# Another order list for all engines and the DMA queue, and one sigmoid ahead of the branch, in an mLSTM + feed-forward kernel

## The chip, the cores and the metric

One core of one Trainium2 chip runs the kernel. The metric is device time in microseconds (us), as the median of runs; lower is better.

## The reference

Two stages follow each other. The first is a gated recurrence over 768 time steps for 4 batches x 8 heads with head size 40: at each step a running maximum `m`, a 40x40 state `C` and a vector `n` are updated and read out.

```
m_new = maximum(f[t] + m, i[t])
C = exp(f[t] + m - m_new) * C + exp(i[t] - m_new) * outer(v[t], k[t])
n = exp(f[t] + m - m_new) * n + exp(i[t] - m_new) * k[t]
y[t] = sigmoid(o[t]) * (C @ q[t]) / maximum(abs(n . q[t]), 1)
```

The second is a feed-forward layer on the 3072 x 320 result: `h = x @ w_in` (320 x 2048), a rational function of each element, `g = (a0 + a1 h + a2 h^2 + a3 h^3) / (1 + |b0||h| + |b1| h^2 + 1e-6)`, and `g @ w_out` (2048 x 320). The weights arrive as 64-bit floats; the kernel splits each of them into a high and a low part on the chip.

## The kernel before

**The work.** The recurrence is cut into 24 units (768 steps in 6 blocks of 128, for each of 4 batches). Two units make one pair, and each pair gives 256 rows of the feed-forward input, a block. There are 12 blocks (n = 0 to 11). The feed-forward work of a block is cut into 8 steps (i = 0 to 7), each with 256 of the 2048 hidden columns. Blocks 0 and 1 are done in two halves: steps 0 to 3 of both, then steps 4 to 7 of both, so that the weights of the second half may arrive later.

**The order.** Every piece of work is registered in a plan with a name, an engine, the names that it reads and writes, and a cost. A text constant, `ORDER`, names all 2723 pieces in one sequence. `plan.listed` turns it into indices and asserts that each piece comes after those it depends on and that no ring of buffers overflows; `plan.issue` then emits them. Within one engine the instructions keep the order of the list (`_Queue` ties each to the one before it), and all loads and nearly all stores go through one DMA queue (SP), in list order too. Across engines only the data dependencies and the reuse of buffers make one wait for another.

**The names.** For a weight chunk `i0..i7`, `o0..o7`, `j0`, `j1` (parts of w_in, w_out, and the last 64 rows of w_in): `raw` is the load; `s0`, `s2`, `o0` are ScalarE steps, `s1`, `s3` VectorE steps, `o2` GpSimd steps of the split; `oc` copies a part of `j` to other partitions through the DMA queue. For a unit u: `lk`, `lq`, `lv` load k, q, v, `lf`, `la` load decay factors that were stored before (units 4 on; units 0 to 3 get them from TensorE, `pf`, `pa`, `pc`); `ogl` loads the output gate and `og` is its sigmoid (ScalarE, three pairs in one go); `kp`, `ke`, `d0`, `d1` are GpSimd, `tk`, `tq`, `S`, `ow` TensorE, `ek`, `eq` ScalarE, `sc` (a scan), `qa`, `P`, `u0`, `u1` VectorE steps. For a pair: `it`, `i1`, `xt` TensorE, `ab`, `xh` ScalarE, `rc`, `x`, `xl` VectorE, `g` GpSimd. For a feed-forward step `n_i`: `f1`, `f2`, `f3` TensorE, `ha`, `u`, `p1`, `y`, `r0` ScalarE, `p3`, `gh`, `m`, `gl` VectorE, `w`, `rm` GpSimd; `ev` and `ed` write the block out. `early` and `gate` are the gate preprocessing (mostly VectorE), of the first 256 time steps and of the rest; `squares`, `lx` and `li` belong to it. `hot` is one of 90 matmuls of the identity by itself, whose results nobody reads. A suffix `.k` is the k-th piece of that name.

**The branch.** The program exists in two variants; a flag is computed from `moe_a` ahead of a branch (`_prologue`, `_decide`), and all of the list is inside the branch. The inputs here take the first variant.

The helper that ties the instructions of a queue has line 34, so nearly all rows of the profile have that line.

Of the kernel before, what the change touches and what calls it, by code (L numbers as in the profile page):

```python
# [147 lines left out]
early early.1 le early.2 early.3 hot hot.1 hot.2 hot.3 hot.4 hot.5 hot.6 hot.7 hot.8 hot.9 hot.10 hot.11 hot.12 hot.13  # L148
hot.14 hot.15 hot.16 hot.17 raw_o1 s2_o1 early.4 zero early.5 early.6 early.7 early.8 early.9 early.10 s0_o1.1
early.11 mc early.12 early.13 early.14 early.15 early.16 early.17 eye1 early.20 early.21 gate.2 gate.4 gate.5 li.2 eye  # L150
s0_o1 s1_o1 s3_o1 li.1 hot.18 s1_o1.1 s3_o1.1 lk_0 pf_0 early.18 raw_i6 gate.6 sc_0 hot.19 hot.20 hot.21 raw_o0 hot.22
pa_0 hot.23 s2_i6 hot.24 hot.25 hot.26 hot.27 s2_o0 s0_o0 o0_o1 s1_o0 hot.28 hot.29 zero.2 s3_o0 s0_o0.1 pa_1 s1_o0.1
s3_o0.1 li.3 lv_0 raw_j1 o2_o1 s0_i6 hot.30 hot.31 hot.32 early.19 ogl_4 gate.3 hot.33 hot.34 ogl_2 s1_i6 squares lx.2
raw_i4 o0_o0 hot.35 hot.36 s0_i4 s2_i4 pc_0 kp_0 tk_0 ke_0 pc_1 s0_j1 s1_i4 o2_o0 hot.37 hot.38 zero.3 s3_i4 o0_i4
ek_0 hot.39 hot.40 hot.41 hot.42 hot.43 zero.1 hot.44 hot.45 hot.46 hot.47 lq_0 hot.48 hot.49 hot.50 raw_o5 hot.51
hot.52 hot.53 hot.54 hot.55 hot.56 o2_i4 hot.57 hot.58 hot.59 hot.60 hot.61 s2_j1 s1_j1 s3_i6 raw_i2 lk_1 raw_j0 s0_o5
kp_1 li s3_j1 ogl_0 o0_i6 s0_o5.1 lq_1 s1_o5 lx.1 hot.62 tq_0 hot.63 s2_o5 eq_0 s1_o5.1 hot.64 o0_j1 hot.65 hot.66
pa_2 ogl_3 o2_i6 lx.3 s3_o5.1 s3_o5 o0_o5 S_0 tk_1 hot.67 qa_0 P_0 P_0.1 lx s0_j0 pc_2 ogl_5 raw_i0 ow_0 pf_1 gate.7
u0_0 ek_1 gate.21 lv_1 hot.68 tq_1 s1_j0 o2_j1 hot.69 hot.70 hot.71 d1_0 ogl_1 lk_2 o2_j1.1 sc_1 s2_j0 s3_j0 eq_1
s0_i2 hot.72 hot.73 hot.74 s2_i2 hot.75 S_1 ke_1 qa_1 o2_o5 o0_j0 o2_j0 raw_i3 u1_0 P_1 s1_i2 P_1.1 hot.76 pf_2 s0_i0  # L160
s1_i0 raw_i1 s2_i0 og_0 o2_j0.1 gate.1 ow_1 gate s3_i2 it_0 s3_i0 u0_1 d1_1 it_0.1 i1_0 hot.77 ab_0 ab_0.1 lq_2 hot.78
hot.79 hot.80 hot.81 sc_2 s0_i3 rc_0 kp_2 u1_1 s1_i3 tk_2 hot.82 g_0 x_0 o0_i0 o0_i2 g_0.1 ke_2 s2_i3 s3_i3 x_0.1
hot.83 hot.84 hot.85 hot.86 hot.87 hot.88 hot.89 ek_2 s2_i1 pf_3 s0_i1 s1_i1 s3_i1 xt_0 o2_i0 oc_j0 xh_0 xl_0 tq_2
eq_2 xh_0.1 o0_i1 o0_i3 S_2 lk_3 xl_0.1 raw_o3 lv_2 kp_3 tk_3 f1_0_0 f1_0_0.1 P_2 P_2.1 ek_3 s0_o3 s2_o3 o2_i1 lf_4
lq_3 ow_2 qa_2 sc_3 o2_i2 ha_0_0 s1_o3 s0_o3.1 pa_3 s3_o3 u0_2 d1_2 ke_3 u_0_0 s1_o3.1 s3_o3.1 p1_0_0 p3_0_0 u1_2
w_0_0 tq_3 eq_3 S_3 P_3 y_0_0 r0_0_0 P_3.1 lk_4 f1_0_1 sc_4 kp_4 tk_4 pc_3 raw_o2 gh_0_0 ek_4 m_0_0 oc_j1 f1_0_1.1
f1_0_2 qa_3 s0_o2 s0_o2.1 raw_i7 rm_0_0 s1_o2 s2_o2 ha_0_1 o2_i3 u_0_1 s1_o2.1 p1_0_1 s0_i7 s3_o2 s2_i7 w_0_1 gl_0_0
s3_o2.1 f2_0_0 f2_0_0.1 lv_3 ow_3 u0_3 p3_0_1 it_1 it_1.1 y_0_1 lq_4 s1_i7 s3_i7 i1_1 f1_0_2.1 d1_3 ke_4 raw_o7 ab_1
ab_1.1 rc_1 f3_0_0 tq_4 r0_0_1 gh_0_1 u1_3 o0_o3 ha_0_2 g_1 x_1 m_0_1 f3_0_0.1 f2_0_1 f1_0_3 gate.8 p1_0_2 g_1.1
p3_0_2 eq_4 x_1.1 rm_0_1 s2_o7 la_4 qa_4 u_0_2 w_0_2 gate.9 gl_0_1 f1_0_3.1 ha_0_3 p1_0_3 raw_i5 lk_5 lf_5 kp_5 d0_4  # L170
S_4 P_4 P_4.1 y_0_2 p3_0_3 f2_0_1.1 f3_0_1 f3_0_1.1 u_0_3 sc_5 r0_0_2 gh_0_2 w_0_3 gate.10 lq_5 tk_5 xt_1 xh_1 la_5
ek_5 m_0_2 xl_1 tq_5 xh_1.1 xl_1.1 rm_0_2 o0_o2 eq_5 qa_5 gl_0_2 ke_5 S_5 P_5 lv_4 ow_4 y_0_3 o0_i7 r0_0_3 u0_4 f1_1_0
P_5.1 gh_0_3 o2_i7 s0_o7 s1_o7 d1_4 u1_4 raw_o4 s0_o4 s2_o4 s3_o7 s1_o4 s0_o7.1 o2_o2 f1_1_0.1 f1_1_1 ha_1_0 o2_o3
f1_1_1.1 s1_o7.1 p1_1_0 s3_o4 s3_o7.1 d0_5 s2_i5 s0_o4.1 f2_0_2 f2_0_2.1 f3_0_2 f3_0_2.1 f2_0_3 m_0_3 rm_0_3 u_1_0
w_1_0 p3_1_0 s1_o4.1 ha_1_1 p1_1_1 u_1_1 s0_i5 gate.11 s3_o4.1 lv_5 lk_6 gate.12 lk_7 gl_0_3 gate.13 f1_1_2 kp_6 w_1_1
p3_1_1 s1_i5 f2_0_3.1 gate.18 s3_i5 f3_0_3 f3_0_3.1 o0_o4 y_1_0 o2_o4 r0_1_0 gh_1_0 pe_0_3 ow_5 pe_0_3.1 u0_5 f1_1_2.1
ha_1_2 m_1_0 tk_6 d1_5 ek_6 f2_1_0 f2_1_0.1 gate.14 gate.15 p1_1_2 u1_5 rm_1_0 gate.16 it_2 it_2.1 gate.19 o0_i5 lq_6
o2_i5 y_1_1 gl_1_0 gate.17 u_1_2 w_1_2 i1_2 p3_1_2 gate.20 ab_2 la_6 ab_2.1 rc_2 r0_1_1 gh_1_1 lf_6 y_1_2 f3_1_0 m_1_1
f1_1_3 f1_1_3.1 ha_1_3 tq_6 sc_6 f3_1_0.1 g_2 x_2 eq_6 r0_1_2 gh_1_2 qa_6 f2_1_1 rm_1_1 u_1_3 p1_1_3 gl_1_1 m_1_2
f2_1_1.1 f1_0_4 f1_0_4.1 f1_0_5 raw_o6 ogl_10 g_2.1 lf_7 ogl_8 o0_o7 s2_o6 ha_0_4 x_2.1 f3_1_1 p1_0_4 p3_1_3 p3_0_4  # L180
ke_6 S_6 P_6 lq_7 w_1_3 f1_0_5.1 f3_1_1.1 P_6.1 u_0_4 y_1_3 rm_1_2 gl_1_2 r0_1_3 s0_o6.1 gh_1_3 kp_7 s1_o6.1 w_0_4
ha_0_5 p1_0_5 m_1_3 gate.24 p3_0_5 s3_o6.1 rm_1_3 gl_1_3 f1_0_6 f2_1_2 f1_0_6.1 f2_1_2.1 u_0_5 w_0_5 y_0_4 ha_0_6
r0_0_4 u_0_6 y_0_5 f3_1_2 f3_1_2.1 f2_1_3 f2_1_3.1 gh_0_4 m_0_4 f3_1_3 f3_1_3.1 r0_0_5 pe_1_3 d0_6 pe_1_3.1 p1_0_6
gate.25 f1_0_7 f1_0_7.1 xt_2 rm_0_4 f2_0_4 gh_0_5 f2_0_4.1 gl_0_4 f3_0_4 ha_0_7 xh_2 xh_2.1 f3_0_4.1 f1_1_4 u_0_7
f2_0_5 f2_0_5.1 p3_0_6 xl_2 xl_2.1 m_0_5 o2_o7 w_0_6 s0_o6 s1_o6 tk_7 f1_1_4.1 s3_o6 y_0_6 p1_0_7 p3_0_7 w_0_7 f1_1_5
f1_1_5.1 rm_0_5 o0_o6 o2_o6 r0_0_6 gh_0_6 gl_0_5 m_0_6 y_0_7 ha_1_4 ek_7 p1_1_4 r0_0_7 p3_1_4 f3_0_5 u_1_4 gh_0_7
gate.22 gate.23 f3_0_5.1 tq_7 f2_0_6 f2_0_6.1 f1_1_6 rm_0_6 gl_0_6 f3_0_6 w_1_4 ha_1_5 p1_1_5 eq_7 y_1_4 m_0_7 rm_0_7
lk_8 lv_6 ogl_9 lq_8 la_7 ogl_6 gate.26 sc_7 qa_7 r0_1_4 gh_1_4 f3_0_6.1 f2_0_7 f2_0_7.1 f1_1_6.1 gl_0_7 u_1_5 ha_1_6
S_7 ke_7 P_7 P_7.1 ow_6 u_1_6 p1_1_6 w_1_5 f3_0_7 f3_0_7.1 m_1_4 p3_1_5 y_1_5 r0_1_5 rm_1_4 ev_0_7 w_1_6 f1_1_7
f1_1_7.1 f1_2_0 ha_1_7 u_1_7 p3_1_6 y_1_6 ev_0_7.1 r0_1_6 gl_1_4 u0_6 kp_8 d1_6 f2_1_4 f2_1_4.1 f3_1_4 f3_1_4.1  # L190
f1_2_0.1 d0_7 gh_1_5 u1_6 m_1_5 gh_1_6 m_1_6 lv_7 gate.27 rm_1_5 gl_1_5 f2_1_5 f2_1_5.1 tk_8 p1_1_7 ha_2_0 u_2_0 w_1_7
w_2_0 ek_8 p1_2_0 p3_1_7 ow_7 u0_7 it_3 d1_7 it_3.1 y_1_7 r0_1_7 p3_2_0 i1_3 y_2_0 f3_1_5 f3_1_5.1 lk_9 lf_8 ogl_11
u1_7 ed_0_7 ogl_7 ed_0_7.1 la_8 ab_3 ab_3.1 f1_2_1 gh_1_7 m_1_7 f1_2_1.1 rm_1_6 gl_1_6 rm_1_7 tq_8 rc_3 f2_1_6
f2_1_6.1 f3_1_6 f3_1_6.1 og_6 gl_1_7 g_3 sc_8 f2_1_7 ke_8 x_3 f2_1_7.1 g_3.1 ha_2_1 p1_2_1 f3_1_7 eq_8 qa_8 u_2_1
w_2_1 r0_2_0 p3_2_1 y_2_1 x_3.1 gh_2_0 S_8 P_8 f3_1_7.1 f1_2_2 f1_2_2.1 kp_9 m_2_0 ev_1_7 r0_2_1 ev_1_7.1 gh_2_1 tk_9
m_2_1 ek_9 ha_2_2 rm_2_0 gl_2_0 p1_2_2 p3_2_2 lq_9 lf_9 rm_2_1 gl_2_1 lv_8 la_9 f1_2_3 f1_2_3.1 ha_2_3 p1_2_3 p3_2_3
tq_9 f2_2_0 eq_9 u_2_2 u_2_3 w_2_2 y_2_2 r0_2_2 qa_9 P_8.1 f2_2_0.1 sc_9 w_2_3 gh_2_2 y_2_3 r0_2_3 m_2_2 f3_2_0 ke_9
lf_10 lk_10 d0_8 f1_2_4 f1_2_4.1 f1_2_5 ha_2_4 f3_2_0.1 rm_2_2 f2_2_1 f1_2_5.1 p1_2_4 ha_2_5 S_9 f2_2_1.1 P_9 P_9.1
f3_2_1 gh_2_3 lv_9 f3_2_1.1 xt_3 f2_2_2 gl_2_2 xh_3 kp_10 xh_3.1 f2_2_2.1 f3_2_2 tk_10 f3_2_2.1 f2_2_3 m_2_3 xl_3
xl_3.1 u_2_4 rm_2_3 ek_10 p1_2_5 w_2_4 gl_2_3 ow_8 ow_9 u0_8 d1_8 p3_2_4 u_2_5 y_2_4 it_4 it_4.1 d0_9 f2_2_3.1 u1_8  # L200
u0_9 p3_2_5 f3_2_3 i1_4 r0_2_4 w_2_5 ab_4 sc_10 gh_2_4 m_2_4 ab_4.1 f1_2_6 y_2_5 r0_2_5 f3_2_3.1 f1_2_6.1 rc_4 ha_2_6
gh_2_5 d1_9 u1_9 g_4 x_4 ed_1_7 ogl_16 rm_2_4 gl_2_4 u_2_6 f2_2_4 f2_2_4.1 p1_2_6 p3_2_6 m_2_5 lk_11 lk_12 f1_2_7
# [1271 lines left out]
```

## Time and profile before

| | us |
|---|---|
| median of 3 runs (501.81 to 502.59) | 501.81 |
| profiled execution | 500.23 |
| span from its first to its last instruction | 498.4 |

The profile is of one execution on the chip. The rows that the prediction rests on stand in a section of their own below.

### The profile page before, as it was taken

How to read it: one execution, taken by the hardware profiler on the slowest of the kernel's cores; microseconds unless marked ns; L12 is line 12 of the kernel's file. 1: busy time of each engine (PE TensorE's matmuls, PEld its weight loads, DVE VectorE, ACT ScalarE, POOL GpSimd, SP SyncE). 2: the span in 40 equal slices, each digit the busy share in tenths (PEclk: the TensorE clock that was granted, in tenths of full speed). 3: DMA queues.
4: the chain of work that ended last, by engine and by line, in shares of the span. 5: the costliest groups of instructions: out<-in, count | busy, mean ns of one | idle time of the engine just before them, and what ended most of it. 6: DMA issues, size and time to landing. Idle time of an engine off the chain costs nothing.

```text
span 498.4 us, 14219 instructions
## 1 busy us (share of the span) xinstructions
PE 478.1 (96%) x5631; PEld 462.1 (93%) x5631; DVE 421.9 (85%) x716; ACT 402.5 (81%) x698; POOL 385.8 (77%) x365
## 2 busy tenths in 40 slices
...
GB/s 181 221 178 238 229 208 177 103 9 71 113 106 77 59 83 101 99 75 83 44 83 87 131 70 57 60 77 15 29 115 62 2 75 3 11 19 1 27 1 35
DMA packets 120158, 42.54 MB, mean 85 GB/s; under 512 B 104338, under 2 KB 112594, under 8 KB 120082
## 3 DMA queue, kind: packets, MB, share of 16 engines
...
## 4 chain that ended last, share of the span: by engine, by line
PE 73%; DVE 7%; ACT 5%; DMA 4%; issue 3%; POOL 3%; SPq 3%; DVEq 0%; ACTq 0%; POOLq 0%
PE ph L34 30%; PE po L34 29%; PE y L34 4%; PE kq L34 3%; PE ow L34 3%; SPq L34 2%; PE ps L34 2%; DMA kr<-in_k_dram 2%; POOL p L34 2%; PE px L34 1%; DMA rawo<-in_moe_w_out_dram 1%; ACT ph L34 1%; DMA rawi<-in_moe_w_in_dram 1%; DVE w L34 1%; DVE gH L34 1%
## 5 line engine op out<-in xcount | busy, mean ns | idle before, releaser
L34 POOL TENSOR_TENSOR p<-p,w 128x512 f32<-128x512 f32 (+1 forms) x97 | 127.8, 1318 | 59.7 <-DVE w L34 55.8
L34 PE MATMUL ph<-xk,wi 128*128 128x256 f32 x1152 | 167.9, 282 | 0.6 <-DVE zo L34 0.5
L34 PEld LDWEIGHTS ph<-xk,wi 128*128 128x128 f32 x1152 | 150.0, 188 | 1.9 <-PE ph L34 0.7
L34 POOL TENSOR_TENSOR w<-w,ha 128x512 f32<-128x512 f32 (+1 forms) x97 | 127.3, 1318 | 9.9 <-ACT w L34 9.9
L34 PE MATMUL po<-wo,gH 128*128 128x320 f32 x768 | 134.6, 312 | 0.0
L34 PEld LDWEIGHTS po<-wo,gH 128*128 128x128 f32 x768 | 115.1, 188 | 0.8
L34 DVE SCALAR_TENSOR_TENSOR gL<-p,ps,ph 128x512 fp32r<-128x512 f32 (+1 forms) x97 | 71.3, 735 | 22.0 <-POOL p L34 19.9
L34 DVE SCALAR_TENSOR_TENSOR w<-w,gH 128x512 f32<-128x512 f32 (+1 forms) x97 | 81.7, 843 | 4.0
L34 ACT ACTIVATE ph<-w,cd 128x512 f32<-128x512 f32 (+1 forms) x97 | 66.6, 687 | 22.6 <-POOL w L34 12.2
L34 DVE SCALAR_TENSOR_TENSOR gH<-p,ps,ph 128x512 fp32r<-128x512 f32 (+1 forms) x97 | 71.3, 735 | 13.8 <-ACT ph L34 12.8
L34 ACT ACTIVATE w<-ha,ba 128x512 f32<-128x512 f32 (+1 forms) x97 | 78.6, 812 | 2.3
L34 ACT ACTIVATE ha<-ph 128x512 f32<-128x512 f32 (+1 forms) x97 | 57.5, 593 | 27.4 <-PE ph L34 26.6
L34 PE MATMUL po<-wo,gL 128*128 128x320 f32 x384 | 77.2, 314 | 0.8 <-DVE gL L34 0.8
L34 DVE SCALAR_TENSOR_TENSOR p<-p,ps,ph 128x512 f32<-128x512 f32 (+1 forms) x97 | 70.5, 734 | 7.2 <-ACT p L34 7.0
L34 ACT ACTIVATE p<-ph,ps 128x512 f32<-128x512 f32 (+1 forms) x97 | 65.3, 680 | 0.3
L34 PEld LDWEIGHTS po<-wo,gL 128*128 128x128 f32 x384 | 59.2, 188 | 2.4 <-DVE gL L34 1.8
L34 ACT ACTIVATE ph<-ph 128x512 f32<-128x512 f32 (+1 forms) x97 | 56.0, 578 | 2.2
L34 PE MATMUL ph<-xk,wY 128*128 128x256 f32 x192 | 53.6, 279 | 0.0
L34 PE MATMUL ph<-xk,wj 128*128 128x256 f32 x192 | 53.4, 278 | 0.0
L34 PEld LDWEIGHTS ph<-xk,wj 128*128 128x128 f32 x192 | 36.2, 188 | 0.0
L34 PEld LDWEIGHTS ph<-xk,wY 128*128 128x128 f32 x192 | 36.1, 188 | 0.0
L34 PE MATMUL hot<-ident 128*128 128x128 f32 x180 | 24.9, 296 | 4.0 <-DVE flag_out L370 4.0
...
## 6 DMA issues: line engine op xcount, KB each, us to landing
rawo<-in_moe_w_out_dram SPq DMA_DIRECT2D x8, 640.0 KB, 6.0
ab<-scrA SPq DMA_DIRECT2D x40, 128.0 KB, 3.6
rawi<-in_moe_w_in_dram SPq DMA_DIRECT2D x8, 512.0 KB, 5.5
...
vb<-in_v_dram SPq DMA_DIRECT2D x48, 80.0 KB, 3.5
og<-in_o_gate_dram SPq DMA_DIRECT2D x48, 80.0 KB, 3.4
...
out_dram<-ot SPq DMA_DIRECT2D x47, 80.0 KB, 2.2
```

The costliest lines, as they stand in the source:

```text
L34: made = fn(*args, **kwargs)
```

## The change

`ORDER` is replaced as a whole by another sequence of the same 2723 pieces: the two lists contain the same words. By its description it was found by a search over scattered transfer times in its first third. Besides, one ScalarE instruction is added in `_prologue`, ahead of the branch: a sigmoid of a single number.

```
@@ -145,168 +145,168 @@
 ORDER = """
-early early.1 le early.2 early.3 hot hot.1 hot.2 hot.3 hot.4 hot.5 hot.6 hot.7 hot.8 hot.9 hot.10 hot.11 hot.12 hot.13
-hot.14 hot.15 hot.16 hot.17 raw_o1 s2_o1 early.4 zero early.5 early.6 early.7 early.8 early.9 early.10 s0_o1.1
...
+raw_o1 lk_0 s0_o1 early eye1 early.1 early.2 le early.3 early.4 early.5 early.6 early.7 early.8 mc hot hot.1 hot.2 hot.3
...
@@ -341,6 +341,7 @@
     make_identity(nc, c["ident"])
     nc.gpsimd.memset(c["cd"][:, 0:1], CD)
+    nc.scalar.activation(pool.tile([1, 1], F32, name="one"), c["cd"][0:1, 0:1], AF.Sigmoid)
     nc.gpsimd.memset(c["qn0"], 0.0)
```

What the two lists give the DMA queue, TensorE and VectorE in the first stretch, read out of the lists (`hot*4`: four of these in a row; `f1_0_0*2`: both pieces of that name):

```
DMA queue (SP), before:
raw_o1 gate lk_0 raw_i6 raw_o0 lv_0 raw_j1 ogl_4 gate ogl_2 raw_i4 lq_0 raw_o5 raw_i2 lk_1 raw_j0 ogl_0 lq_1 ogl_3
ogl_5 raw_i0 lv_1 ogl_1 lk_2 raw_i3 raw_i1 gate*2 lq_2 oc_j0 lk_3 raw_o3 lv_2 lf_4 lq_3 lk_4 raw_o2 oc_j1 raw_i7 lv_3
lq_4 raw_o7 la_4 raw_i5 lk_5 lf_5 lq_5 la_5 lv_4 raw_o4 lv_5
DMA queue (SP), after:
raw_o1 lk_0 gate raw_i4 lq_0 raw_j0 ogl_0 lk_1 raw_o0 raw_o5 lv_0 lq_1 lk_2 ogl_2 ogl_4 lv_1 raw_i6 ogl_3 ogl_5 ogl_1
lq_2 raw_i0 raw_j1 lk_3 raw_i1 oc_j0 gate lq_3 raw_i3 raw_i2 lv_2 gate raw_o2 oc_j1 lv_3 lf_4 lk_4 raw_o3 gate raw_i7
lq_4 raw_o4 lv_4 lk_5 la_4 lv_5 raw_i5 lq_5 lk_6 lf_5 la_5

TensorE, before:
hot*19 pf_0 early hot*4 pa_0 hot*7 pa_1 hot*7 tk_0 hot*26 tq_0 hot*4 pa_2 S_0 tk_1 hot*1 ow_0 pf_1 hot*1 tq_1 hot*7
S_1 hot*1 pf_2 ow_1 it_0*2 i1_0 hot*5 tk_2 hot*8 pf_3 xt_0 tq_2 S_2 tk_3 f1_0_0*2 ow_2 pa_3 tq_3 S_3 f1_0_1 tk_4
f1_0_1 f1_0_2 f2_0_0*2 ow_3 it_1*2 i1_1 f1_0_2 f3_0_0 tq_4 f3_0_0 f2_0_1 f1_0_3*2 S_4 f2_0_1 f3_0_1*2 tk_5 xt_1 tq_5
S_5 ow_4
TensorE, after:
hot*16 early pf_0 pa_0 pa_1 tk_0 hot*5 tq_0 hot*5 S_0 hot*2 pf_1 hot*3 tk_1 ow_0 pa_2 pa_3 hot*1 tq_1 hot*2 S_1 tk_2
hot*5 ow_1 it_0 hot*1 pf_2 it_0 i1_0 tq_2 hot*10 S_2 hot*5 xt_0 hot*1 pf_3 tk_3 hot*4 f1_0_0*2 tq_3 hot*9 S_3 hot*9
ow_2 hot*2 f1_0_1*2 hot*3 f1_0_2*2 hot*2 ow_3 hot*3 it_1*2 i1_1 hot*2 f2_0_0*2 f3_0_0 f1_0_3*2 f3_0_0 tk_4 f2_0_1*2
f3_0_1 xt_1 f3_0_1 tq_4 f2_0_2*2 f1_1_0*2 f3_0_2*2 f1_1_1*2 S_4 f2_0_3 tk_5 f2_0_3 ow_4

VectorE, before:
early*5 zero early*7 mc early*6 eye1 early*2 gate*2 s1_o1 s3_o1 s1_o1 s3_o1 gate sc_0 s1_o0 s3_o0 s1_o0 s3_o0 s1_i6
squares lx s1_i4 s3_i4 s1_j1 s3_i6 s3_j1 s1_o5 lx s1_o5 lx s3_o5*2 qa_0 P_0*2 lx gate u0_0 gate s1_j0 sc_1 s3_j0 qa_1
u1_0 P_1 s1_i2 P_1 s1_i0 s3_i2 s3_i0 u0_1 sc_2 rc_0 u1_1 s1_i3 x_0 s3_i3 x_0 s1_i1 s3_i1 xl_0*2 P_2*2 qa_2 sc_3 s1_o3
s3_o3 u0_2 s1_o3 s3_o3 p3_0_0 u1_2 P_3*2 sc_4 gh_0_0 m_0_0 qa_3 s1_o2*2 s3_o2 gl_0_0 s3_o2 u0_3
VectorE, after:
early eye1 early*8 mc early*11 gate*2 s1_o1 s3_o1 gate lx*2 zero sc_0 s1_o1 s3_o1 s1_i4 s3_i4 qa_0 P_0*2 s1_o0*2 s3_o0
sc_1 s3_o0 lx u0_0 lx gate u1_0 s1_j0 s3_j0 gate qa_1 gate P_1 s1_o5 P_1 gate s1_o5 gate u0_1 s3_o5*2 gate*3 u1_1
s1_i6 gate*2 s3_i6 sc_2 rc_0 qa_2 x_0 s1_i0 s3_i0 P_2 x_0 gate P_2 s1_j1 s3_j1 xl_0 sc_3 xl_0 s1_i1 s3_i1 gate squares
qa_3 s1_i3 gate*2 P_3 p3_0_0 gate s1_i2 s3_i2 P_3 u0_2 s3_i3 u1_2 gh_0_0 m_0_0 s1_o2 gate s3_o2 s1_o2 s3_o2 gl_0_0
p3_0_1 u0_3
```

In both lists all 90 `hot` come before the first `f2`. After the first stretch the two lists go on in different sequences too, with the same structure: block after block, with the units of later blocks in between.

## Rows read from the trace of the kernel before

**Rows 1.** The page: busy time, share of the span and instructions by engine.
```profile
PE 478.1 (96%) x5631; PEld 462.1 (93%) x5631; DVE 421.9 (85%) x716; ACT 402.5 (81%) x698; POOL 385.8 (77%) x365
```

**Rows 2.** Busy time by stretch; columns PE, PEld, DVE, ACT, POOL, clock, DMA share, GB/s.
```profile
4.00:20.00 16.00, 15.50 (x179) 14.78 (x180) 14.54 (x47) 7.76 (x14) 6.88 (x14) 1.00 0.87 210
20.00:40.00 20.00, 17.02 (x280) 15.60 (x280) 16.87 (x31) 15.07 (x27) 14.72 (x14) 1.00 0.98 205
40.00:58.00 18.00, 16.07 (x295) 14.62 (x291) 14.75 (x29) 16.54 (x29) 11.13 (x14) 1.00 1.01 250
58.00:100.00 42.00, 38.53 (x529) 35.77 (x527) 41.44 (x84) 38.47 (x72) 36.85 (x34) 1.00 0.90 169
```

**Rows 3.** Waits of TensorE from 80 us to the end: total, times, longest.
```profile
PE po L34 <- DVE gL L34: 0.8, 2, 0.4
```

**Rows 4.** Timeline of TensorE: the first two matmul groups of block 1, and `xt_2`.
```profile
76.95 0.95 PE L34 MATMUL ph<-xk,wi 128*128 128x256 f32 x6
...
108.45 0.82 PE L34 MATMUL px<-ident,xn 128*128 128x128 f32 x6
```

**Rows 5.** The chain that ended last: unbroken runs of matmuls (start, us, count).
```profile
269.68 3.78 PE ph L34 x32
...
442.48 4.11 PE po L34 x28
```

**Rows 6.** Timeline of TensorE: an unbroken run of `hot`.
```profile
19.58 5.97 PE L34 MATMUL hot<-ident 128*128 128x128 f32 x52
```

**Rows 7.** DMA issues by operand: number, KB of each, median us to landing.
```profile
rawo<-in_moe_w_out_dram SPq DMA_DIRECT2D x8, 640.0 KB, 6.0
...
rawi<-in_moe_w_in_dram SPq DMA_DIRECT2D x8, 512.0 KB, 5.5
...
vb<-in_v_dram SPq DMA_DIRECT2D x48, 80.0 KB, 3.5
...
fb<-scrF SPq DMA_DIRECT2D x20, 128.0 KB, 3.2
```

**Rows 8.** Timeline of the DMA queue: its first issue in the branch.
```profile
4.18 0.40 SPq L34 DMA_DIRECT2D rawo<-in_moe_w_out_dram  x1
```

**Rows 9.** Timeline of ScalarE: its first use of that load.
```profile
8.54 0.81 ACT L34 ACTIVATE zo<-rawo 128x640 f32<-128x640 f32 x1 [3.41 <-DMA rawo<-in_moe_w_out_dram]
```

**Rows 10.** Busy time as in Rows 2, up to the scan of unit 5.
```profile
4.00:71.56 67.56, 61.27 (x926) 56.89 (x927) 59.41 (x132) 52.43 (x94) 43.06 (x51) 1.00 0.99 218
```

**Rows 11.** Timeline of VectorE: `squares`, two of `lx`, a wait, and `sc_5`.
```profile
19.85 1.52 DVE L34 SCALAR_TENSOR_TENSOR ps<-pa,ps 128x1 f32<-128x1 f32 x1
...
28.01 0.28 DVE L34 TENSOR_TENSOR gate_x<-gate_f,gate_m 32x128 f32<-32x128 f32 x1
...
30.40 2.46 DVE L34 TENSOR_TENSOR gate_x<-gate_f,gate_m 32x128 f32<-32x128 f32 x1
...
43.94 0.17 DVE L34 TENSOR_SCALAR na<-y 128x16 f32<-128x16 f32 x1 [1.47 <-ACT y L34]
...
71.56 1.22 DVE L34 TENSOR_TENSOR_SCAN e<-g,eye 128x512 f32<-128x512 f32 x1
```

**Rows 12.** Timeline of GpSimd beside these.
```profile
19.82 1.54 POOL L34 TENSOR_TENSOR wo<-zo,wo 128x640 fp32r<-128x640 f32 x1
...
30.21 1.27 POOL L34 TENSOR_TENSOR wi<-zi,wi 128x512 fp32r<-128x512 f32 x1
31.45 1.26 POOL L34 TENSOR_TENSOR wY<-zj,wj 64x512 fp32r<-64x512 f32 x1
```

**Rows 13.** Timeline of ScalarE around its first sigmoid.
```profile
3.85 1.28 ACT L34 ACT_TABLE_LOAD   x1 [3.85 <-DVE flag_out L370]
...
40.37 1.28 ACT L34 ACT_TABLE_LOAD   x1 [0.48 <-issue]
41.66 1.99 ACT L34 ACTIVATE og<-og 128x640 f32<-128x640 f32 x3
43.55 0.35 ACT L34 ACTIVATE y<-y 128x8 f32<-128x8 f32 x2
```

More of the change, by code (lines that the diff above doesn't have):

```diff
@@ L147 @@
 ORDER = """
[L148 to L202, printed above, removed]
```

270 lines of the change are left out of this document (163 added, 107 removed).

## The prediction

> **What bounds the kernel now.** I read the page first, then busy time by stretch, then the waits of TensorE. TensorE is busy for 96% of the span [rows 1], and from 80 us on it waits only 0.8 us in all [rows 3]. So whatever TensorE is late by at about 80 us, the whole kernel is late by at its end, and what a new order can win lies ahead of that.
>
> How late is it? I added up the matmuls in list order with durations from unbroken runs: 3.78 us for 32 of `ph` is 0.118 each [rows 5], so a piece `f1` of eight takes 0.94; 4.11 for 28 of `po` is 0.147, so an `f2` piece of four takes 0.59 and an `f3` piece of two 0.29; 5.97 for 52 instructions of `hot` [rows 6], two to a piece, is 0.23 a piece. Attention pieces I took likewise (0.45 to 1.1 each). Ahead of `f1_1_0`, the first matmul of block 1, the list has 59.6 us of TensorE work, 20.7 of it `hot`, and it starts at 76.95: 17.4 late. Ahead of `xt_2` it has 89.6, and that starts at 108.45 [rows 4]: 18.8 late. From there it no longer grows visibly.
>
> Of the 18.8, about 4 pass ahead of the branch (first load in it at 4.18 [rows 8]). The rest is VectorE's doing. From 58 to 100 us VectorE is busy for 41.44 of 42.00 us; before it is not: 14.54 of 16, 16.87 of 20, 14.75 of 18 [rows 2]. It has idled 7.8 us by 58, and then runs flat out until TensorE's queue is fed. VectorE has slightly more to do than TensorE in this part: with pitches from its timeline (a scan 1.15, a `p3` or `gl` 0.66, a `P` 0.34, a split piece 0.4 to 0.62) the old list has 87.3 us of VectorE work that must end before `f1_0_6`, with 82.4 of TensorE work ahead of it, 4.9 more. I scale by 1.03, because up to `sc_5` the pitches give 57.7 and the profile 59.41 [rows 10]; the excess is then 7.5. Branch 4.0, excess 7.5 and idle time 8.15 (below) make 19.7, which is 0.9 above the 18.8 that is measured. I take that as the error of this sum.
>
> **Why VectorE idles.** The loads. Add up the KB on the DMA queue in list order (640 for a `raw_o`, 512 for a `raw_i` or `raw_j`, 160 for `lk`, `lq`, `lv`, `ogl`, 256 for `lf`, `la`, `oc`; [rows 7]). `sc_5` needs `lf_5`, and 13,763 KB end with it. The queue moved 218 GB/s up to then at a share of 0.99 [rows 10], 213 KB of 1,024 bytes per us. The first load, 640 KB from 4.18, was used at 8.54 [rows 8, 9]: 3.0 for the bytes and 1.4 more. So `sc_5` can start at 4.2 + 64.6 + 1.4 = 70.2; it started at 71.56 [rows 11]. VectorE had worked 59.41 of the 67.56 us from 4.00 [rows 10]: 8.15 idle. The loads explain it to 1.4 us.
>
> **The change, part by part.** (1) The list moves every piece and removes none, so bytes and instructions stay. I asked of each list where VectorE first needs more bytes than have come. In the old one the excess of bytes/212 over VectorE work ahead grows to 7.2 us, at `u0_3` and `sc_5`. In the new one its largest value is 0.4, at `u0_0`: that needs `lv_0`, the eleventh piece on the queue, 3,872 KB, with 17.8 us of VectorE work ahead (44 pieces; 54 with 23.8 us in the old list). At 213 KB per us it can start at 4.2 + 18.2 + 1.4 = 23.8, plus about 1 for its `ow_0` on TensorE; VectorE would be there at 4.0 + 18.3 = 22.3. That makes 1.5 to 2.5 us idle, and after it every load comes at least 1.2 us (`s1_i7`) ahead of need by the same count. Two things make room: unit 5 comes later against VectorE's work (`sc_5` has 69.5 us of it ahead, not 57.7), and 19 instead of 5 `gate` pieces (8.0 us instead of 2.5) run ahead of `u0_3` where the old list waits for bytes.
>
> So the idle time by this part falls from 8.15 to 2.0 if only loads count. The upper end is 8.15, as now, if other waits (such as the 1.47 us for ScalarE at 43.94 [rows 11]) fill the gap. I take 4.4, below the middle of 2.0 and 8.15, because most waits of the old list sit inside time in which the loads were missing anyway: a gain of 3.75.
>
> (2) The excess of VectorE over TensorE work is nearly the same: 81.0 against 76.0 at `ow_5`, 67.1 against 62.0 at `S_4`; scaled, 7.4 at `ow_5`. Gain 0.1, taken as 0. TensorE's own loads bind less: `f1_0_0` needs `oc_j0`, 7,776 KB, so 42.1 us, with 32.2 of work ahead: 9.9 late, under the 15.8 left over from VectorE (4.0 + 7.4 + 4.4).
>
> (3) DMA queue. A store and a load that reads it come closer: `lf_4` stands four pieces behind the store of the early factors instead of six. If the store lands like the transfers of [rows 7], in 3.2 to 6.0 us, and the three pieces between (five issues) take at least 0.4 each [rows 8], SP stands there for 0 to 4.0 us. The loads behind it have 1.2 us in hand, and 2.4 more where VectorE idles 4.4 and not 2.0, so I count 0, and 0.4 at most.
>
> (4) After the first stretch both lists feed a TensorE that does not wait [rows 3]. I count 0, with 1 us either way for the ending.
>
> (5) The sigmoid. ScalarE idles until 3.85, and its first load of a function table falls there; the next, 1.28 us, comes at 40.37 ahead of the first `og`, whose successor `y` VectorE then waited for [rows 11, 13]. With a sigmoid ahead of the branch the second may be dropped, since Copy, Abs, Identity and Square run after it from the same table. Bounds: 0, if the branch loads its own tables again, and 1.28, all inside the idle time that (1) already counts. The added instruction itself hides in ScalarE's 3.85 us; uncovered it would cost a load, 1.28. I count 0. The sigmoid starts 0.01 us after the 1.28 of its load, with 0.48 ahead of the load at most [rows 13]. The Trainium skill (ScalarE: Activation LUTs, section What ACT_TABLE_LOAD costs) puts a switch at about 2.66 us, load and drain; these rows show no drain of that size, and by the page the upper bound would be 2.66.
>
> Sum: 3.75 off. The profiled execution took 500.23, which gives 496.5; it lies 1.6 below the median of the runs, 501.81, and I forecast the median: **498.1**. Its own range is 495.7 (idle 2.0 us, a gain of 6.15) to 500.8 (idle 7.2, a gain of 1.0).
>
> **Rivals.** *Nothing gained:* VectorE idles 8 us as before, for other engines instead of loads. For it: the new list hands work to and fro more often (`P_1 s1_o5 P_1 gate s1_o5`). Against it: GpSimd was busy 32.7 and ScalarE 39.4 of the first 54 us [rows 2], so both have room. Time 501.8.
>
> *Slower, by stretched VectorE instructions.* One `lx` took 2.46 us where another took 0.28; it ended at 32.86, when two GpSimd instructions from 30.21 had just ended at 32.71. A line of `squares` took 1.52, from 19.85 to 21.37, beside a GpSimd instruction from 19.82 to 21.36 [rows 11, 12]. Both read two operands of SBUF. The new list pairs other instructions. Four `lx`, four lines of `squares`, the early steps and the `m` pieces can be hit at 1.3 to 2.2 each; two are hit now, for 3.5 together. With three more at 2.2 the forecast becomes 498.1 + 6.6 = 504.7; it decides from two more on (4.4 takes all of the gain). Against it: in the new list two of the `lx` come right behind `gate.6`, before GpSimd has begun the long `o2` pieces (1.3 to 1.5 us each) that they met now. The Trainium skill (SBUF — State Buffer, section SBUF: two separate sides) says that VectorE with two SBUF inputs and GpSimd hold one port pair in turn, for a whole instruction; these rows agree. By that rule it counts which instructions run side by side, and my sums of bytes and work leave that out.
>
> *More gained:* idle 2.0 and the 1.28 of the table load on top: 501.8 - 6.15 - 1.28 = 494.4.
>
> **How the numbers follow.** Forecast 0.64; nothing gained 0.13; stretched, slower 0.17; more 0.06. About 0.2%, 1.0 us, is what a measurement of this kernel can tell from no change. Faster: 0.64 + 0.06 = 0.70; same 0.13; slower 0.17. The range runs from 495.3, which leaves out the larger gains, to 502.6, which takes in "nothing gained" and a single extra stretch and leaves out most of the slower case: 0.2 in all.
>
> **What the next profile would show.** Right: VectorE idle under 5 us between 4 and 58 us, its longest wait for PE `ow` (behind `vb`) near 24 us; `f1_1_0` before 73 us although the work ahead of it is 57.6 instead of 59.6; `xt_2` (98.7 of work ahead) at about 113 to 114; TensorE without waits after 80. One table load fewer, none ahead of the first `og`. Wrong: VectorE's first 58 us idle as before; `lx` or `squares` of over 1 us in greater number; waits of TensorE after 100 us; or SP standing at `lf_4` while the DMA share falls below 0.9 between 20 and 80 us.

## The result, and the profile after

| us | before | after |
|---|---|---|
| median of the runs | 501.81 | 508.30 (507.28 to 508.64) |
| profiled execution, its span | 500.23, 498.4 | 507.28, 504.9 |

The ratio is 1.0133, 95% interval 1.0098 to 1.0167. The forecast was 498.1, the range ended at 502.6: the change made the kernel slower, and by more than the forecast's slower rival.

Busy time of the changed kernel by stretch, columns as in [rows 2]:

```profile
4.00:20.00 16.00, 14.68 (x215) 13.74 (x217) 14.73 (x45) 6.85 (x14) 6.64 (x11) 1.00 1.00 244
20.00:40.00 20.00, 16.28 (x334) 14.52 (x328) 17.32 (x38) 14.82 (x28) 13.38 (x18) 1.00 0.92 170
40.00:58.00 18.00, 17.29 (x214) 16.42 (x208) 17.25 (x36) 16.68 (x29) 13.42 (x13) 1.00 1.01 247
58.00:100.00 42.00, 37.45 (x495) 35.00 (x494) 41.17 (x70) 36.40 (x68) 34.51 (x32) 1.00 0.58 144
```

VectorE idles 54.00 - 14.73 - 17.32 - 17.25 = 4.70 us by 58 us, against 7.84 in [rows 2]. So the first step happened. What came of it is in the timeline of TensorE, to set beside [rows 4]:

```profile
72.65 0.97 PE L34 MATMUL ph<-xk,wi 128*128 128x256 f32 x6
...
118.37 0.82 PE L34 MATMUL px<-ident,xn 128*128 128x128 f32 x6
```

With the work ahead that the prediction counted, `f1_1_0` is 72.65 - 57.6 = 15.0 us late (17.4 before), and `xt_2` 118.37 - 98.7 = 19.7 (18.8 before). A lead of 2.4 us at 73 us has become a lag of 0.9 at 118. The waits of TensorE from 80 us on say how, and that it goes on (columns as in [rows 3], where 0.8 us was all):

```profile
PE ow L34 <- DVE pm L34: 2.1, 1, 2.1
PE ph L34 <- DVE qA L34: 1.4, 1, 1.4
PE ph L34 <- DVE st L34: 0.9, 1, 0.9
PE po L34 <- DVE gL L34: 0.8, 2, 0.6
PE y L34 <- DVE st L34: 0.6, 1, 0.6
PE kq L34 <- DVE qA L34: 0.6, 1, 0.6
PE y L34 <- DVE gL L34: 0.6, 1, 0.6
PE ph L34 <- DVE xk L34: 0.2, 1, 0.2
```

All of them wait for VectorE. What VectorE did just then, in its timeline (`sc_5`, the product that TensorE's 1.4 us waited for, a `p3`, and `gate.25`):

```profile
79.83 2.87 DVE L34 TENSOR_TENSOR_SCAN e<-fb,eye 128x512 f32<-128x512 f32 x1
...
84.15 0.68 DVE L34 TENSOR_TENSOR qA<-kq,ab 104x512 f32<-104x512 f32 x1
...
91.21 0.74 DVE L34 SCALAR_TENSOR_TENSOR p<-p,ps,ph 128x512 f32<-128x512 f32 x1
...
92.20 2.96 DVE L34 TENSOR_TENSOR_SCAN gate_f<-gate_x,gate_f 128x128 f32<-128x128 f32 x1
```

And GpSimd beside it:

```profile
79.09 2.52 POOL L34 TENSOR_TENSOR w<-w,ha 128x512 f32<-128x512 f32 x2
...
91.14 2.52 POOL L34 TENSOR_TENSOR w<-w,ha 128x512 f32<-128x512 f32 x2
93.63 1.25 POOL L34 TENSOR_TENSOR wi<-zi,wi 128x512 fp32r<-128x512 f32 x1
```

The scan of unit 5 took 1.22 us before [rows 11]. Here it starts inside a pair of GpSimd instructions that ends at 81.61, and it ends 1.09 us after that, at 82.70: it stood still until GpSimd was through. `gate.25` stood until three had ended at 94.88, and TensorE's `ow` waited behind it. The `p` at 91.21 runs beside the same pair in its usual 0.74; it reads `ph`, which TensorE's matmuls write (PSUM), and so one tensor from SBUF at most. The Trainium skill (SBUF — State Buffer, section SBUF: two separate sides) states this: a VectorE instruction with two SBUF inputs and a GpSimd one exclude each other for a whole instruction, and whichever starts first goes first. These rows agree with the first half. With the second they do not, by the starts that the profile gives: the scan began at 79.83, the second of the two GpSimd instructions (1.26 us each) at about 80.35, and the scan waited for that one too. The share of 41.17 of 42.00 us "busy" above has 1.65 + 2.55 us of such standing still in it; a busy engine need not be a working one.

Farther on the same thing: `sc_18` in VectorE's timeline, GpSimd beside it, and TensorE behind it.

```profile
310.56 2.82 DVE L34 TENSOR_TENSOR_SCAN e<-g,eye 128x512 f32<-128x512 f32 x1
```
```profile
309.77 2.53 POOL L34 TENSOR_TENSOR w<-w,ha 128x512 f32<-128x512 f32 x2
```
```profile
314.40 0.83 PE L34 MATMUL ph<-xk,wi 128*128 128x256 f32 x5 [0.94 <-DVE st L34]
```

Such instructions are not peculiar to the new list. The kernel before has them too, `m_3_3` and `sc_22` in its VectorE timeline, beside GpSimd pairs from 194.34 to 196.87 and from 398.12 to 400.66:

```profile
194.35 3.07 DVE L34 SCALAR_TENSOR_TENSOR w<-w,gH 128x512 f32<-128x512 f32 x1
...
398.89 2.86 DVE L34 TENSOR_TENSOR_SCAN e<-fb,eye 128x512 f32<-128x512 f32 x1
```

No listed wait of TensorE follows either: the two of [rows 3] lie behind 486 us. By these rows a stretched instruction need not cost time; it does where TensorE's next work stands behind it.

A different kind stands ahead of 195 us: the two `qa` of a pair, on GpSimd, directly behind each other, with a `rm` behind them, and VectorE's `gl` waiting for that `rm`.

```profile
188.03 2.99 POOL L34 TENSOR_TENSOR qA<-qT,ab 104x512 f32<-104x512 f32 x2
190.99 1.28 POOL L34 TENSOR_TENSOR p<-p,w 128x512 f32<-128x512 f32 x1
```
```profile
192.30 0.75 DVE L34 SCALAR_TENSOR_TENSOR gL<-p,ps,ph 128x512 fp32r<-128x512 f32 x1 [2.06 <-POOL p L34]
```

ScalarE around the added sigmoid, against [rows 13]:

```profile
0.74 1.28 ACT L344 ACT_TABLE_LOAD   x1 [0.74 <-PEq L1459]
2.03 0.20 ACT L344 ACTIVATE one<-cd 1x1 f32<-1x1 f32 x1
...
35.20 1.99 ACT L34 ACTIVATE og<-og 128x640 f32<-128x640 f32 x3 [2.04 <-DMA og<-in_o_gate_dram]
```

No load stands ahead of the first `og` any more; it waits for its data instead. The sigmoid again follows its load by 0.01 us.

### The profile page after: what moved, and what is told of

Same layout as the page of the kernel before. It is cut to its first block, busy times and chain, and to the rows that moved or that the text cites. A ratio compares the mean times of both kernels' runs of the same rounds, so it can differ in the third digit from the quotient of the medians.

```text
span 504.9 us, 14189 instructions
## 1 busy us (share of the span) xinstructions
PE 479.8 (95%) x5631; PEld 461.5 (91%) x5631; DVE 427.6 (85%) x716; ACT 401.0 (79%) x698; POOL 381.3 (76%) x365
## 4 chain that ended last, share of the span: by engine, by line
PE 66%; DVE 12%; POOL 5%; issue 3%; ACT 2%; DMA 1%; DVEq 0%; POOLq 0%; ACTq 0%; SPq 0%
PE ph L34 27%; PE po L34 25%; PE y L34 4%; PE kq L34 3%; DVE w L34 3%; DVE gH L34 2%; POOL p L34 2%; PE ow L34 2%; PE ps L34 2%; POOL w L34 1%; DVE gL L34 1%; DVE p L34 1%; DMA rawo<-in_moe_w_out_dram 1%; PE hot L34 1%; DVE e L34 1%
## 5 line engine op out<-in xcount | busy, mean ns | idle before, releaser
L34 POOL TENSOR_TENSOR p<-p,w 128x512 f32<-128x512 f32 (+1 forms) x97 | 125.9, 1298 | 58.1 <-DVE w L34 55.5
L34 PE MATMUL po<-wo,gH 128*128 128x320 f32 x768 | 137.6, 313 | 0.0
L34 DVE SCALAR_TENSOR_TENSOR w<-w,gH 128x512 f32<-128x512 f32 (+1 forms) x97 | 84.8, 874 | 4.0 <-POOL p L34 0.5
L34 ACT ACTIVATE ph<-w,cd 128x512 f32<-128x512 f32 (+1 forms) x97 | 66.7, 688 | 23.8 <-DVE p L34 15.8
L34 ACT ACTIVATE ha<-ph 128x512 f32<-128x512 f32 (+1 forms) x97 | 57.1, 589 | 24.7 <-PE ph L34 23.8
L34 PE MATMUL hot<-ident 128*128 128x128 f32 x180 | 26.6, 299 | 4.0 <-DVE flag_out L371 4.0
```

What stands on the lines that cost most here:

```text
L34: made = fn(*args, **kwargs)
```

## The experiments

Theory: after about 75 us the new order pairs long VectorE instructions of two SBUF operands with runs of GpSimd instructions, and places GpSimd pairs badly, and such places make TensorE late. Rivals: the sigmoid; the new first third hands on a state that costs time whatever follows; the work itself is too much for VectorE there.

In this table, TensorE's lateness (start of the piece's second half in the profiled execution less the matmul work ahead of it, prices as in the prediction) and the timed ratio to the kernel before, run beside it on the same chip:

| kernel | f1_1_0 | f1_0_6 | f1_2_6 | f1_3_7 | f1_7_2 | f1_11_6 | ratio |
|---|---|---|---|---|---|---|---|
| before | 17.4 | 18.8 | 19.2 | 19.9 | 20.5 | 21.2 | |
| after | 15.0 | 19.7 | 21.0 | 22.8 | 25.6 | 27.4 | 1.0133 |
| e1, old list and sigmoid | 19.1 | 20.4 | 20.9 | 21.5 | 21.9 | 22.6 | 0.9985 |
| e2, new to 535 | 15.5 | 24.3 | 24.7 | 25.6 | 26.1 | 26.8 | 1.0063 |
| e3, new to 865 | 14.9 | 21.1 | 23.8 | 24.3 | 24.7 | 25.5 | 1.0112 |
| e4, old to 865, then new | 19.3 | 20.1 | 21.1 | 22.9 | 25.8 | 27.2 | 1.0125 |
| e5, new, two scans moved | 15.2 | 18.0 | 19.2 | 20.9 | 23.8 | 25.5 | 1.0104 |
| e6, four moves | 19.1 | 21.8 | 23.1 | 23.9 | 30.8 | 31.6 | 1.0119 |
| e13, five moves | 15.2 | 18.0 | 19.2 | 20.0 | 22.3 | 24.3 | 1.0063 |
| e8, new to 730 | 15.9 | 22.1 | 24.8 | 25.3 | 25.7 | 26.8 | 1.0077 |
| e7, two scans moved, to 730 | 15.7 | 18.5 | 21.3 | 22.0 | 22.4 | 23.4 | 1.0015 |
| e9, more moved, to 836 | 17.8 | 20.7 | 21.4 | 21.9 | 22.3 | 23.0 | 0.9958 |
| e10, two scans moved, to 988 | 15.0 | 17.8 | 19.0 | 19.5 | 20.0 | 20.7 | 0.9977 |
| e12, old, gate.25 moved | 19.7 | 21.2 | 22.7 | 23.3 | 23.9 | 24.7 | 1.0018 |

The first columns of one and the same list differ from execution to execution (the old one 17.4 to 19.7 at `f1_1_0`); the growth from `f1_2_6` on hardly does.

**e1, the sigmoid alone.**

```
 make_identity(nc, c["ident"])
 nc.gpsimd.memset(c["cd"][:, 0:1], CD)
+nc.scalar.activation(pool.tile([1, 1], F32, name="one"), c["cd"][0:1, 0:1], AF.Sigmoid)
```


> The old list with only the sigmoid of a single number added ahead of the branch. Theory (the new list does the harm, the sigmoid none): 500.5 to 502 us, the lower end if the table load that falls away ahead of the first og was on the path. Rival (the sigmoid or its table load delays the branch): 505 us or more, with the first matmul in the branch more than 1 us later than in the kernel before.

Measured: 501.87 us beside 502.85, ratio 0.9985 (0.9962 to 1.0007). Eight table loads in all instead of nine, and no delay of the branch. The sigmoid is not the cause, and gives nothing that can be measured.

**e2, e3, e8: the new list up to a point, then the old order.** The diff shows the seam; e3 is cut behind `ev_1_7 p3_2_1`, e8 behind `f3_0_6.1 d0_6`.

```
 f1_1_2.1 gl_1_0 s2_i5 s3_i5
-f1_1_3 o2_o4 pe_0_3.1 f1_1_3.1 f1_0_4 d0_5
+s2_o7 S_5 P_5 P_5.1 s0_o7 s1_o7
...
```


> The new list up to its piece 535 (shortly behind f1_1_2, about 84 us), then all remaining pieces in the old order; the sigmoid stays. In the changed kernel TensorE is 15.4 us late at f1_1_2 by its own list, against 18.1 in the kernel before, so the head is 2.7 ahead. Theory (the harm lies in the order after the first stretch, where VectorE scans meet GpSimd instructions): the old order keeps most of that lead, less the 1.4 us that TensorE waits after the scan of unit 5, which stays: 499.1 to 500.8 us. Rival (the new head hands over a state that costs time later whichever order follows): 505 to 508 us.

> The new list up to its piece 865 (ev_1_7.1, about 140 us), then the old order; the sigmoid stays. Both stretched scans of the changed kernel, that of unit 5 and that of the gate, are inside. TensorE was 21.0 us late at f1_2_6 in the changed kernel and 19.2 in the one before. Theory (each stretch of the order brings its own waits): 501.8 + 1.8 = 503.6 us, and of the waits of TensorE after 150 us those at 193, 195, 269 and 314 us are gone. Rival (the later waits follow from the first third): 507 to 508.5 us.

> The changed kernel's list unaltered up to its piece 730 (about 120 us), and all that remains in the old order. Theory: TensorE is 19.5 us late there (18.5 in the kernel before), and the old order adds 2.7: 1.0 above the kernel before, 502.8 us, and 3 to 3.5 us above the same list with the two scans moved. Rival (the seam or the state costs more): 505 to 508 us.

Measured: 506.12 (1.0031 to 1.0096), 506.96 (1.0073 to 1.0150), 505.89 (1.0049 to 1.0106). By the time alone the rivals come out ahead in all three. The table says otherwise: from `f1_2_6` to the end they grow by 2.1, 1.7 and 2.0 us, as the kernel before does (2.0), not by 6.4, and in e3 the waits at 193, 195, 269 and 314 us are gone. The loss has two places. One is the seam, where pieces that TensorE wants at once come before their inputs: it waits 2.2 us for `ow_5` in e2, 0.9 for `S_8` in e3, 0.7 and 1.2 for `tk_7` and `ow_6` in e8, and in e2 its clock fell with that (last section). So a splice has a price of its own, and I should have priced it. The other place, in e3 and e8, lies ahead of the seam: TensorE waits 2.1 us behind the stretched `gate.25` as in the changed kernel, but here its clock falls after that wait, and at `f1_0_6` it is 21.1 and 22.1 late where the changed kernel, with the same list up to there, is 19.7.

**e4, the reverse: the old list up to 865, then the new order.**

```
 f1_2_2 f1_2_2.1 kp_9 m_2_0
-ev_1_7 r0_2_1 ev_1_7.1 gh_2_1 tk_9 m_2_1
+gate.32 ogl_22 gate.31 ogl_23 gate.29 lf_9
...
```

(Minus: how the old list goes on.)

> The old list up to its piece 865 (about 140 us), then the remaining pieces in the new order; the sigmoid stays. Theory (each stretch of the order brings its own waits): the new order adds 6.5 us of lateness from f1_2_6 to the end, the old one 2.1, so 501.8 + 4.4 = 506.2 us. Rival (the later waits follow from the first third): 501 to 502.5 us.

Measured: 507.86 (1.0091 to 1.0159). Growth from `f1_2_6` to the end 6.1. The new order's waits come back behind a first third that is the old one. TensorE's waits from 100 us on in e4:

```profile
PE po L34 <- DVE gL L34: 1.2, 3, 0.6
PE ph L34 <- DVE st L34: 1.0, 1, 1.0
PE y L34 <- DVE st L34: 0.6, 1, 0.6
PE y L34 <- DVE gL L34: 0.6, 1, 0.6
PE ph L34 <- DVE xk L34: 0.2, 1, 0.2
```

The rival of the state handed on falls: that part of the loss belongs to the order after the first third. Nor is the work there too much for VectorE. From `f1_2_6` to `f1_11_6`, in the kernel before and in the changed one (columns as in [rows 2]):

```profile
163.86:476.28 312.42, 312.26 (x3490) 305.31 (x3489) 259.62 (x401) 258.99 (x443) 252.46 (x227) 1.00 0.29 58
165.65:482.46 316.81, 314.17 (x3490) 305.34 (x3489) 261.84 (x398) 257.00 (x440) 247.99 (x226) 1.00 0.26 55
```

VectorE is busy for 83% of either. Of the 4.4 us that the new order takes longer, 2.5 are time in which TensorE stands still (2.64 against 0.16); the other 1.9 are in its busy time, and these rows do not say where.

**e5, two scans moved in the new list.**

```
-gl_0_3 y_1_0 r0_1_0 sc_5 w_1_1 f2_0_3.1 ow_4 u0_4 p3_1_1 gh_1_0 tq_5
+gl_0_3 y_1_0 r0_1_0 w_1_1 f2_0_3.1 ow_4 u0_4 p3_1_1 gh_1_0 sc_5 tq_5
...
-P_5 gate.25 P_5.1
+P_5 P_5.1
...
-gh_1_3 m_1_3 ab_2.1
+gh_1_3 m_1_3 gate.25 ab_2.1
```


> The changed kernel with two VectorE scans moved a few places back in its list: sc_5 from in front of u0_4 to behind gh_1_0 (three instructions later), gate.25 from between the two P_5 to behind m_1_3. In the changed kernel they started beside two GpSimd instructions in a row and took 2.87 and 2.96 us where such scans took 1.22 and 0.41 in the kernel before; TensorE then waited 1.37 and 2.10 us. Theory (the stretched scans make TensorE wait): both scans below 1.7 us, the two waits together below 0.8 us, TensorE 2.7 to 3.5 us earlier at f1_0_6, and the time 3 us under that of the changed kernel: 504.5 to 505.5 us. Rival (the work in that stretch is too much for VectorE wherever the scans stand, or the lead is given back later): waits of the same size elsewhere and 507 to 508.5 us.

Measured: 506.50 (1.0055 to 1.0154). VectorE's timeline:

```profile
82.63 1.22 DVE L34 TENSOR_TENSOR_SCAN e<-fb,eye 128x512 f32<-128x512 f32 x1
...
98.41 0.41 DVE L34 TENSOR_TENSOR_SCAN gate_f<-gate_x,gate_f 128x128 f32<-128x128 f32 x1
```

The same two scans at 1.22 and 0.41 us. TensorE's wait of 2.10 is gone, the other is 0.80. At `f1_0_6` it is 1.7 us earlier, at the end 1.9: the theory holds, at a little over half the size I gave it. These are figures of the profiles; the interval of the times overlaps that of the changed kernel (1.0098 to 1.0167). The last two thirds still add 6.3.

**e7, the two scans moved, new up to 730, then old** (the seam of e8):

> The changed kernel's list with the two scans moved, up to its piece 730 (f1_1_6.1, about 120 us), and all that remains in the old order. Theory (a lead at 120 us is kept by the old order, which adds 2.7 us of lateness from there): TensorE 16 us late at f1_1_6 instead of 18.5 in the kernel before, so 2.5 under the kernel before: 499.3 us, and faster than both kernels. Rival (the old order meets other pairs of VectorE and GpSimd instructions when it starts from another state): 502 to 506 us.

Measured: 503.15 (0.9992 to 1.0037), against 505.89 for e8 on the same chip. The two scans are worth 2.7 us there, with what the clock lost behind their wait in e8 (22.1 late at `f1_0_6`, here 18.5). The seam takes the lead (18.4 late at `f1_1_5`, 20.6 at `f1_1_7`), so my 499.3 was a miss.

**e6 and e13, moves in the last two thirds.** e6 has the two moves and these; e13 has the last one as well.

```
-u_6_5 w_6_4 sc_18 w_6_5
+u_6_5 w_6_4 w_6_5
...
-u1_17 gh_6_4 f2_6_3.1
+u1_17 gh_6_4 sc_18 f2_6_3.1
...
-y_3_2 qa_10 qa_11 rm_3_1
+y_3_2 qa_10 rm_3_1
...
-ek_12 d0_11 f2_3_1
+ek_12 d0_11 qa_11 f2_3_1
...
-w_6_6 lf_20 lq_18 w_6_7
+w_6_6 lq_18 lf_20 w_6_7
```


> As the experiment with two scans moved, and two more moves in the last two thirds: sc_18 (2.82 us beside two GpSimd instructions, TensorE then waits 0.94) from behind u0_17 to behind gh_6_4, and qa_11, a GpSimd product, from directly behind qa_10 to behind d0_11 (the two took 2.99 us, gL then waited 2.06 for GpSimd, and TensorE 0.16 and 0.61). Theory: the waits of TensorE near 193, 195 and 314 us go, 1.7 us by the waits and about 2.4 by the growth of lateness there (f1_3_4 to f1_3_6 and f1_6_4 to f1_6_7 added 1.4 and 1.4); the time 1.7 to 2.8 us under that of the experiment with two moves: 502 to 503.5 us. Rival (each wait moves to the next piece): within 0.7 us of the two moves.

Measured: 508.25 (1.0077 to 1.0160): not the gain I expected. (By the times it cannot be told from e5: four runs each, 506.10 to 510.98 here, 504.61 to 508.48 there.) The move of `qa_11` did what it should, 1.3 us of growth from `f1_3_4` to `f1_3_7` (e5) became 0.5. The move of `sc_18` cured the scan and made a wait that was not there. The DMA queue and TensorE in e6:

```profile
317.07 1.11 SPq L34 DMA_DIRECT2D g<-scrF  x2
318.27 0.54 SPq L34 DMA_DIRECT2D qn<-in_q_dram  x1
```
```profile
323.69 1.06 PE L34 MATMUL kq<-ident,qn 128*104 128x128 f32 x4 [3.14 <-DMA qn<-in_q_dram]
```

`sc_18` frees the buffer that `lf_20` fills. The scan ended at 317.04, `lf_20` went out at 317.07, and `lq_18`, which needs no such buffer, stood behind it on the in-order queue. In the changed kernel the same two issues were at 313.41 and 314.61. Behind the wait TensorE's clock fell, too (0.62 from 324 to 328 us), which is part of the growth of 6.9 us up to `f1_7_2`.

> The four moves again, with one more: on the DMA queue the load lf_20 stands behind lq_18 instead of ahead of it. With the four moves lf_20 waited for its buffer, which sc_18 frees, went out at 317.07 instead of 311.61, and lq_18 behind it reached TensorE 3.14 us late. Theory (the move of sc_18 was right, and the queue behind the freed buffer took the gain): no wait for a load after 300 us, lateness growing by at most 0.6 us from f1_6_4 to f1_7_2 (1.5 with two moves), and 2.0 to 2.6 us under the list with two moves (25.5 us late at the end): 23 to 23.5 us late. Rival (TensorE waits there whatever the place of sc_18): growth of 1.4 us or more there.

Measured: 505.10 (1.0041 to 1.0085). No wait for a load is left, and growth from `f1_6_4` to `f1_7_2` is 0.4 us (21.9 to 22.3) instead of 1.7 in e5. At the end TensorE is 24.3 late, 1.2 under e5 and not 2.0 to 2.5. Of the 0.9 us won by `qa_11` at `f1_3_7`, 0.7 had come back by `f1_4_2`; of the 1.5 at `f1_7_2`, 0.6 by `f1_7_5`, in part as a wait for the next VectorE piece. Waits of TensorE in e13 between 180 and 480 us:

```profile
PE ph L34 <- DVE xk L34: 0.6, 1, 0.6
PE y L34 <- DVE gL L34: 0.6, 1, 0.6
```

Both come behind a stretched `m`, which reads two tensors in SBUF as well and takes 0.69 us elsewhere. VectorE and GpSimd, `m_5_2` and `m_7_0`:

```profile
264.40 2.00 DVE L34 SCALAR_TENSOR_TENSOR w<-w,gH 128x512 f32<-128x512 f32 x1
...
330.01 2.19 DVE L34 SCALAR_TENSOR_TENSOR w<-w,gH 128x512 f32<-128x512 f32 x1
```
```profile
264.56 1.30 POOL L34 TENSOR_TENSOR w<-w,ha 128x512 f32<-128x512 f32 x1
...
329.10 2.56 POOL L34 TENSOR_TENSOR w<-w,ha 128x512 f32<-128x512 f32 x2
```

The `gl` and the `xl` that TensorE waits for (0.57 us at 267.12, 0.59 at 333.52) come directly behind the first and one instruction behind the second.

**e10 and e9, better seams.** e10 has the two moves; e9 has `gate.25` moved as in e5, and these, with `qa_7` placed ahead of `m_1_6`:

```
-r0_1_0 sc_5 w_1_1 f2_0_3.1 ow_4 u0_4 p3_1_1 gh_1_0 tq_5 eq_5 ke_5 qa_5 m_1_0 d1_4 u1_4
+r0_1_0 w_1_1 f2_0_3.1 ow_4 p3_1_1 u0_4 tq_5 eq_5 d1_4 qa_5 gh_1_0 u1_4 sc_5 ke_5 m_1_0
```


> The new list with the two scans moved, up to its piece 988 (u1_9, about 158 us), then the old order. Theory: TensorE is 19.2 us late at f1_2_6 as in the kernel before, and the old order adds 2.0 from there: within 0.5 us of the kernel before, 3.5 to 4.5 us under the list with two scans moved alone, whose last two thirds added 6.3. Rival (the last two thirds cost 6 whichever list, once the first third is new): 4 to 5 us above the kernel before.

> The new list up to its piece 836 (f3_1_6.1, about 136 us), with gate.25 behind m_1_3 and the pieces behind ow_4 in the order p3_1_1 u0_4 tq_5 eq_5 d1_4 qa_5 gh_1_0 u1_4 sc_5 ke_5 m_1_0, so that qa_5 no longer stands behind the scan sc_5, and with qa_7 in front of m_1_6; then the old order. Theory: with two scans moved TensorE was 17.7 us late at f1_1_6; without the 0.80 us that it waited there for qa_5, 16.9, against 18.5 in the kernel before; the old order adds 2.7 from there. So 1.5 us under the kernel before. Rival (the seam costs as much as the seam at piece 730 did, 2.9 us there): 1 to 2 us above the kernel before.

Measured: e10 500.82 (0.9957 to 0.9997), e9 500.10 (0.9935 to 0.9981), both beside 502.38. e10 goes as the new list to `f1_2_6` (19.0 late) and from there as the old one (1.7 more). The best version is thus new in the first third, with its scans moved, and old behind it: e9 is 0.4% under the kernel before by the ratio, e10 0.2%. (The row of e9 is of an execution whose clock fell, see the last section.)

**e12, the reverse test in the kernel before.**

```
-m_0_4 d0_6 pe_1_3.1 p1_0_6 gate.25
+m_0_4 d0_6 pe_1_3.1 p1_0_6
...
-xl_2.1
+xl_2.1 gate.25
```


> The kernel before (no sigmoid, old list) with one piece moved: gate.25, the scan that took 0.41 us, from behind m_0_4 to behind xl_2.1, where two GpSimd instructions in a row ran from 109.91 to 112.91 in the kernel before and VectorE came to at 110.94. Theory (a VectorE scan of two operands in SBUF does not run beside GpSimd): it takes 1.5 to 2.4 us there, with the same data and the same shape. Rival (the scan took long in the changed kernel for another reason, its data or a load): 0.4 us. The time: 0 to 2 us above the kernel before, as TensorE has work queued there.

Measured: 503.61 (0.9994 to 1.0041). VectorE and GpSimd:

```profile
53.34 1.21 DVE L34 TENSOR_TENSOR_SCAN e<-fb,eye 128x512 f32<-128x512 f32 x1
...
113.50 0.47 DVE L34 TENSOR_TENSOR_SCAN gate_f<-gate_x,gate_f 128x128 f32<-128x128 f32 x1
113.90 1.71 DVE L34 SCALAR_TENSOR_TENSOR w<-w,gH 128x512 f32<-128x512 f32 x1
```
```profile
51.77 2.54 POOL L34 TENSOR_TENSOR wi<-zi,wi 128x512 fp32r<-128x512 f32 x2 [0.88 <-ACT wi L34]
...
112.40 2.66 POOL L34 TENSOR_TENSOR w<-w,ha 128x512 f32<-128x512 f32 x2
```

A miss: the scan took 0.47. It came where the first of the two GpSimd instructions was about to end and got in between them. The next VectorE instruction with two SBUF operands, an `m` of 0.69 elsewhere, took 1.71 and ended 0.55 after the pair. So meeting a pair is a risk and not a certainty. The scan at 53.34 is that of unit 3, whose `fb` TensorE wrote into PSUM: one SBUF operand, beside GpSimd to 54.31, and 1.21 us.

## Why the prediction was wrong, point by point

The step that failed is (4): "After the first stretch both lists feed a TensorE that does not wait [rows 3]. I count 0, with 1 us either way for the ending." I read a row of the old list and gave it to both. The old order adds 2.0 us from `f1_2_6` to the end, the new one 6.4 (6.1 in e4, behind an old first third). Even for the old list the row says too little: its waits are 0.8 us, and yet lateness grows from 18.8 at `f1_0_6` to 21.2, where I wrote that it "no longer grows visibly". Of my signs of being wrong, the one that came was waits of TensorE after 100 us.

(1), idle time: right in the main. 7.84 us became 4.70 by 58 us (I took 4.4), and TensorE was 2.4 less late at `f1_1_0`, of the 3.75 that I forecast. My place for VectorE's longest wait was wrong: it was 1.67 us at 37.48, for ScalarE, whose `og` waited for its load, and not for `ow` near 24.

(2), the excess of VectorE over TensorE as before: wrong, in good part by the stretched scans. From `f1_1_0` to `f1_0_6` lateness grew by 4.7 us (1.4 before); without the two stretches by 2.8 (e5).

(3), the queue: right. `lf_4` went out at 50.82, 1.0 us after the issue before it had ended. The DMA share was 0.91 from 20 to 80 us; from 58 to 80 it was 0.83, under my mark of 0.9, but VectorE was busy for 21.57 of those 22 us. (5), the sigmoid: right, one load fewer, nothing in the time.

The rival that won, *slower by stretched VectorE instructions*, had 0.17, and its 504.7 was 3.6 too low. Its mechanism was right and its list too short: it named `lx`, `squares`, the early steps and `m`, and priced three more hits. In the first 58 us the new list was kinder: four `lx` took 0.28 each (one took 2.46 before [rows 11]), `squares` 0.62 (1.52). The scans `sc` and `gate.25` were not on the list, though they read two SBUF operands too and are the longest of these instructions, and nothing was counted behind 100 us, where the `m` that it did name cost time as well (e13). By its own rule I should have gone through the whole list.

In sum, in lateness: 2.4 won by 73 us, 3.3 lost by `f1_0_6`, 5.3 after it; 6.2 together, and the spans differ by 6.5. Shown by experiment: the two scans (1.7 to 2.7), `qa_11` and `sc_18` (1.2 at the end). The other 3.1 us between e13 and the kernel before belong to the new order behind the first third, by e4 and e10. The waits behind two stretched `m` are 1.2 of them, read from the trace and not tested by a move; what makes the other 1.9 stays open. `m` pieces of 0.882 us on average in the changed kernel against 0.851, 3.0 us over 95 of them, are a candidate that is only argued.
